# A hand-ordered head for a chunk-selecting attention kernel: first loads as float32 by the SyncE queue, rounding on chip, and zero matmuls on TensorE

## The chip, the cores and the metric

The kernel runs on one core of a Trainium2 chip. A core has five engines with an instruction queue each: TensorE (PE, matmuls; its weight loads are shown as PEld), VectorE (DVE), ScalarE (ACT), GpSimd (POOL) and SyncE (SP). Engines run side by side and wait for one another by semaphores; each engine takes its own instructions in order. DMAs are issued from a queue of POOL or of SP and run on sixteen DMA engines. SBUF is the on-chip memory with 128 partitions, PSUM the memory that matmuls write.

The metric is the time of one execution in microseconds on the device. Before the change the median of three runs is 209.1 us (208.97 to 209.35).

## The reference

Four batches of eight heads, 768 positions, head size 64, all inputs float32. The first half is attention in which each query sees at most six chunks of 32 keys; the second half is a gated MLP over the joined heads.

```python
k_min, k_max = min/max of k over each chunk of 32           # 24 chunks
ub   = sum_d max(q*k_min, q*k_max)                          # upper bound of each query against each chunk
ub   = where(chunk of the query >= chunk, ub, -1e9)
top  = the 6 chunks of largest ub
s    = q @ k.T / 8, kept where the chunk is selected and the key is not later, else -1e9
attn = softmax(s) @ v                                       # per head
x    = heads joined: (4, 768, 512)
h = relu(x @ w_in); u, v = halves of h
v = normalise(v) over its 512 features; v = w_spatial @ v + b_spatial (over positions)
out = (u * v) @ w_out                                       # (4, 768, 512) float32
```

## The kernel before

Two heads make a *pair*; there are 16 pairs, four for each batch. All on-chip operands are float16: the loads of `q`, `k` and `v` go through POOL's DMA queue, which casts from float32 on the way (`load_k`, `load_q`, `load_v`, L318 to L345). A *group* `g` is two pairs that are loaded together; the first group's `k` and `q` are loaded pair by pair (L329, L338), all later ones in one DMA for both pairs (L327, L336).

For each pair the work has these steps, by the names in the code:

- `k_transpose` (L170, six PE transposes, out `kTp`), `k_max` and `k_min` (L178, L182, DVE reductions to 24 chunk bounds), `k_bounds` (L189, two small copies `km<-kmm`), `k_operand` (L194, two copies of the transposed keys into half of `kh`; the other half of `kh` holds a constant pattern, `expand`, that `init_kh` (L150) writes once into each of the eight `kh` tiles).
- `q_transpose` (L205, five PE transposes, out `trm` or `tr`), `q_parts` (L210 and L212 or L214: positive and negative part of q, out `rq`), `bounds` (L219 and L222: `ub`, with the causal mask `later` added by a matmul), `top` (L232: ten MAX8), `select` (L237: writes "not selected" flags into `qs` beside q).
- `a_transpose` and `a_copy` (L251, L257): for each of the two heads, q and flags transposed into the moving operand `a`.
- `scores` (L266, and in batch 0 the diagonal mask `tri` by L269), `e` (L271: exp on ACT), `values` (L289), `normalise` (L296, L297), `x_transpose` (L310, L311). Each pair has two heads of six score tiles: twelve exps, ten of 512 columns and two of 128.

The MLP of a batch runs among the pairs of the next batch (`mlp`, L388 and around).

The order of the work is set by *beats*: `at(beat, step)` puts a step on a list, twelve beats to a pair, and the steps are traced beat by beat. A scheduler then orders each engine's instructions by its own estimates, but inside `tc.manual_schedule` the engines that are named keep the traced order. Before the change this holds for PE alone and for the beats below 6. Beat `B0` (-30) holds the initial work: the first loads, the constants and the whole chain of pair 0 up to its first scores. `p` is pair 0, `n` pair 1. DMAs, POOL's work and everything on DVE and ACT are ordered by the scheduler.

The first work on each queue before the change is, in order: POOL issues two `k` DMAs (pair 0), makes `identity` (L116), issues two `q` DMAs (pair 0), two `k` DMAs (pair 1), makes the masks `later` and `tri` (L140 to L145), and issues the `q` DMAs of pair 1, `v` of group 0, and then `k`, `q`, `v` of group 1. DVE sets zeros (`qs` of all three groups, `km`, `eps_t`, ones in `vt`), then makes `expand` (L132) and `sub_chunk` (L135), and waits for `kTp`. ACT loads its table, writes four of the constant halves of `kh`, works for pair 0, and writes the other four. SP has nothing to do before 60 us.

PSUM: `ml_tile` and `trans_tile` of batch 0 share three buffers of the pool `ps_ml`; `sc` has three buffers of its own.

Of the kernel before, what the change touches and what calls it, by code (L numbers as in the profile page):

```python
# [16 lines left out]
P = 128  # L17
# [31 lines left out]
def kernel(  # L49
# [62 lines left out]
    eps_t = cp.tile([P, 1], F32)  # L112

# [5 lines left out]
    def init_ring(i):  # L119

        nc.vector.memset(qs_ring[i][:, :, :, 0:4:3, :], 0.0)

    def init_small():
        nc.vector.memset(km_ring[0], 0.0)
        nc.vector.memset(km_ring[1], 0.0)
        nc.vector.memset(eps_t, 1e-6)
        for t in v_ring:
            nc.vector.memset(t[:, :, :, D:D + 2], 1.0)

# [8 lines left out]
    def init_masks():  # L138

        nc.gpsimd.memset(later, 0.0)  # L140
# [3 lines left out]
        nc.gpsimd.memset(tri, 0.0)  # L144
# [3 lines left out]
    def init_kh(i):  # L148
        for hi, (d0, d1) in enumerate(HALF):
            nc.scalar.copy(kh_ring[i][hi][d0:d1, :], expand)  # L150
# [6 lines left out]
    class Pair:  # L157
# [27 lines left out]
        def k_bounds(self):  # L185
            for hi, (d0, d1) in enumerate(HALF):
                copy = nc.gpsimd.tensor_copy if 2 <= self.i < 4 else nc.scalar.copy
                s0, s1 = HALF[1 - hi]
                copy(self.km[d0:d1, :, hi], self.kmm[s0:s1])  # L189
# [12 lines left out]
        def q_transpose(self):  # L202
            self.tr = self.trans_tile()
            for t in range(1, NQT):
                nc.tensor.transpose(self.tr[:, t * P:(t + 1) * P], self.qs[:, t, 1:3, :], identity)  # L205

        def q_parts(self, m):
            if m == 0:
                self.rq = sb.tile([P, 2, S], F16, tag="rq", name="rq")
                nc.vector.tensor_scalar(self.rq[:, 0, P:S], in0=self.tr[:, P:S], scalar1=0.0, scalar2=None, op0=Alu.max)  # L210
            elif self.i < 1:
                nc.scalar.activation(self.rq[:, 1, P:S], self.tr[:, P:S], func=Act.Relu, scale=-1.0)  # L212
# [40 lines left out]
        def a_copy(self, hi):  # L253
            if self.i >= 8:
                return
            copy = nc.vector.tensor_copy if self.i < 2 and hi == 0 else nc.scalar.copy
# [60 lines left out]

    def load_k(g, hi, xy=None):  # L318
# [7 lines left out]
        if xy is None:  # L326
            nc.gpsimd.dma_start(out=t[:, :, :, 1 - hi, :].rearrange("p x t d -> p (x t) d"), in_=source(k, b, h, 2))  # L327
        else:
            nc.gpsimd.dma_start(out=t[:, xy, :, 1 - hi, :], in_=source(k, b, h + xy, 1))  # L329

    def load_q(g, hi, xy=None):
# [3 lines left out]
        if xy is None:  # L335
            nc.gpsimd.dma_start(out=t.rearrange("p x t d -> p (x t) d"), in_=source(q, b, h, 2))  # L336
        else:
            nc.gpsimd.dma_start(out=t[:, xy], in_=source(q, b, h + xy, 1))  # L338

    def load_v(g):  # L340
        b, hp = divmod(2 * g, HP)
        t = v_ring[g % 3]
        nc.gpsimd.dma_start(out=t.rearrange("p h t c -> p (h t) c")[:, :, 0:D], in_=source(v, b, 2 * hp, 4))
# [10 lines left out]
    def load_w_in(j):  # L354
        for hi in range(2):
            r = (4 * (j // 2) + j % 2 + 2 * hi) * D
            nc.gpsimd.dma_start(out=w_in_sb[hi * D:(hi + 1) * D, j], in_=moe_w_in[r:r + D, :])
# [96 lines left out]
    at(B0, load_k, 0, 0, 0)  # L454
    at(B0, load_k, 0, 1, 0)
    at(B0, init_identity)
    at(B0, load_q, 0, 0, 0)
    at(B0, load_q, 0, 1, 0)
    at(B0, init_ring, 0)
    at(B0, init_small)  # L460
    at(B0, init_expand)
    at(B0, load_k, 0, 0, 1)
    at(B0, load_k, 0, 1, 1)
    at(B0, init_masks)
    at(B0, load_q, 0, 0, 1)
    at(B0, load_q, 0, 1, 1)
    at(B0, load_v, 0)
    at(B0, init_ring, 1)
    at(B0, init_ring, 2)
    at(B0, init_kh, 0)  # L470
    at(B0, init_kh, 1)
    at(40, load_b)
    for g in range(1, NPAIR // 2):
        t0 = 2 * g * BEATS
        for hi in range(2):
# [3 lines left out]
    for i, p in enumerate(pairs):  # L479
        t0 = i * BEATS  # L480
        for hi in range(2):
            for g in range(len(TILES)):
                at(t0 + 6 * hi + g, p.scores, hi, g)
# [6 lines left out]
    for i, p in enumerate(pairs):  # L490
# [3 lines left out]
        t0 += 4 if i < 4 else 0  # L494
        at(t0 - (22 if i < 4 else 27), p.k_transpose)
# [16 lines left out]
    p, n = pairs[0:2]  # L512
    for beat, *step in (
            (B0 + 1, p.k_transpose), (B0 + 1, p.k_max), (B0 + 1, p.k_min), (B0 + 1, p.k_operand, 0),
            (B0 + 1, p.q_transpose), (B0 + 1, p.q_parts, 0), (B0 + 1, p.k_bounds),
            (B0 + 1, p.q_parts, 1), (B0 + 1, p.k_operand, 1), (B0 + 1, p.bounds), (B0 + 1, p.top, 0),
# [78 lines left out]
```

The softmax here doesn't subtract the row's maximum and nothing guards it: scores larger than these inputs give would overflow.

## Time and profile before

| What | us |
|---|---|
| median of three runs | 209.1 (208.97 to 209.35) |
| the profiled execution, its own time | 208.6 |
| span of that execution, first to last instruction | 206.9 |
| busy in the span: PE / DVE / ACT / POOL | 187.8 / 154.5 / 158.1 / 80.5 |
| first transposes of pair 0 on PE start | 5.75 |
| first exp starts | 15.29 |
| copies of `a` of pair 3 on ACT start (36 exps are done) | 37.91 |
| first MLP activation on ACT starts | 57.10 |

The span is 1.7 us shorter than the execution's time, and the execution is 0.5 us below the median. A busy PE is not a PE at its peak, since matmuls are pipelined and their ends are modelled. In a line of instructions the columns are start, length, engine, line of the code, operation, output and inputs with their shapes, and in brackets the idle time before it with what ended it. In a line of the chain of work that ended last they are start, length, and what it was.

### The profile page before, as it was taken

The page shows a single profiled execution, that of the slowest core. Times are in us where ns is not written, and L with a number is a line of the kernel's source. Part 1 is how long each engine was busy: PE and PEld are TensorE (multiplying, and loading weights), DVE is VectorE, ACT ScalarE, POOL GpSimd, SP SyncE. Part 2 cuts the span into 40 slices and gives each one's busy share as a digit, 9 for nine tenths or more (in the row PEclk, how much of TensorE's full clock was granted, in tenths as well). Part 3 has the DMA queues.
Part 4 walks back from the last instruction along what each step waited for, and adds up shares of the span by engine and source line. Part 5 has one row for each costly group of instructions (what it writes and reads, how often), then busy time and mean ns, then how long its engine had stood idle before and what let it go on. Part 6 is the DMA issues. An engine that isn't in the chain of part 4 may idle for free.

```text
span 206.9 us, 5068 instructions
## 1 busy us (share of the span) xinstructions
PE 187.8 (91%) x1922; PEld 115.1 (56%) x1922; DVE 154.5 (75%) x454; ACT 158.1 (76%) x326; POOL 80.5 (39%) x100
## 2 busy tenths in 40 slices
PE   0368999898899999999999999999999999999992
PEld 0266776775666665656655656565555454444440
DVE  6467979989799989899797999887647456365520
ACT  4797989899998889785989996669999830666042
POOL 7997659596992463236114111111111110000000
PEclk9999999999999999999999999999999999999999
DMA  5999999999999999979998926648782124540356
GB/s 38 92 118 154 140 178 158 173 177 167 177 162 162 97 119 128 135 130 147 149 278 153 180 62 57 127 88 158 181 166 65 38 29 92 187 152 3 72 128 256
DMA packets 114424, 27.27 MB, mean 132 GB/s; under 512 B 109536, under 2 KB 110816, under 8 KB 114400
## 3 DMA queue, kind: packets, MB, share of 16 engines
q0 software_dynamic: 76544, 12.20, 89.8%
q1 hardware_dynamic: 37856, 14.75, 36.4%
q8 instruction: 15, 0.25, 0.5%
q14 instruction: 9, 0.07, 0.1%
HBM read 24.38 MB, written 6.29 MB: 148 GB/s over the span
## 4 chain that ended last, share of the span: by engine, by line
PE 69%; ACT 17%; DVE 8%; issue 2%; DMA 2%; POOL 0%; DVEq 0%; ACTq 0%; POOLq 0%
PE mlp L388 40%; PE sc L266 12%; ACT e L271 10%; PE acc L289 7%; PE kTp L170 2%; ACT a L257 2%; DVE kmm L178 2%; PE ub L222 2%; DMA k<-in_k_dram 2%; PE trm L251 2%; ACT vraw L398 1%; PE tr L205 1%; DVE vn L412 1%; DVE kmm L182 1%; ACT u L420 1%
## 5 line engine op out<-in xcount | busy, mean ns | idle before, releaser
L271 ACT ACTIVATE e<-sc 128x512 f16<-128x512 f32 x192 | 96.9, 553 | 14.8 <-PE sc L266 13.4
L266 PE MATMUL sc<-a,kh 128*128 128x512 f16 (+3 forms) x256 | 65.5, 308 | 2.1 <-ACT e L271 1.5
L388 PE MATMUL mlp<-w_in_sb,xT 128*128 128x512 f16 x192 | 53.0, 379 | 0.1
L278 POOL TENSOR_SCALAR_AFFINE_SELECT e<-e 128x768 f16<-128x768 f16 x24 | 20.9, 869 | 66.3 <-ACT e L271 66.3
L289 PEld LDWEIGHTS <-e 128*128 128x128 f16 x672 | 31.4, 97 | 17.0 <-DVE x L297 3.8
L388 PE MATMUL mlp<-vn,wsT 128*128 128x512 f16 x144 | 37.3, 379 | 0.0
L289 PE MATMUL acc<-vt,e 128*128 128x65 f16 x672 | 35.3, 193 | 0.7 <-DVE x L297 0.4
L266 PEld LDWEIGHTS <-kh 128*128 128x128 f16 x256 | 22.7, 98 | 13.3 <-issue 0.8
L437 ACT COPY o<-mlp 128x512 f32<-128x512 f32 x24 | 14.1, 586 | 19.5 <-PE mlp L388 19.1
L400 DVE BATCH_NORM_STATS2 stats<-vraw 128x6 f32<-128x512 f32 x24 | 16.6, 693 | 12.9 <-ACT vraw L398 12.5
L388 PE MATMUL mlp<-w_out_sb,gT 128*128 128x512 f16 x96 | 25.1, 379 | 0.0
L388 PEld LDWEIGHTS <-xT 128*128 128x128 f16 x192 | 17.2, 97 | 12.6 <-issue 0.4
L427 DVE SCALAR_TENSOR_TENSOR g<-mlp,b_col,u 128x512 f16<-128x512 f32 x24 | 17.9, 748 | 7.3 <-PE mlp L388 6.2
L232 DVE MAX8 max<-ub 128x8 f32<-128x8 f32 (+4 forms) x160 | 15.6, 165 | 5.1 <-PE ub L222 4.9
L388 PEld LDWEIGHTS <-wsT 128*128 128x128 f16 x144 | 12.9, 98 | 10.4
L178 DVE TENSOR_REDUCE kmm<-kTp 128x24 f16<-128x768 f16 x16 | 15.2, 948 | 3.7 <-PE kTp L170 2.7
L297 DVE TENSOR_TENSOR x<-acc,rec 128x384 f16<-128x384 f32 x32 | 17.6, 551 | 0.4
L336 POOL DMA_DIRECT2D qs<-in_q_dram x14 | 14.6, 1049 | 5.9 <-PE sc L266 5.9
L194 DVE COPY kh<-kTp 64x768 f16<-64x768 f16 x30 | 16.5, 549 | 0.5
L398 ACT ACTIVATE vraw<-mlp 128x512 f32<-128x512 f32 x24 | 14.4, 601 | 3.0 <-PE mlp L388 3.0
L420 ACT ACTIVATE u<-mlp 128x512 f16<-128x512 f32 x24 | 14.3, 598 | 1.7 <-PE mlp L388 1.5
L327 POOL DMA_DIRECT2D k<-in_k_dram x14 | 14.4, 1045 | 2.5 <-PE kTp L170 1.8
(67 smaller groups left out, 230.2 us busy)
## 6 DMA issues: line engine op xcount, KB each, us to landing
out_dram<-o SPq DMA_DIRECT2D x24, 256.0 KB, 2.3
vt<-in_v_dram POOLq DMA_DIRECT2D x8, 384.0 KB, 8.8
k<-in_k_dram POOLq DMA_DIRECT2D x14, 192.0 KB, 8.1
qs<-in_q_dram POOLq DMA_DIRECT2D x14, 192.0 KB, 7.5
ws_raw<-in_moe_w_spatial_dram POOLq DMA_DIRECT2D x6, 192.0 KB, 6.9
w_in_sb<-in_moe_w_in_dram POOLq DMA_DIRECT2D x8, 128.0 KB, 6.9
w_out_sb<-in_moe_w_out_dram POOLq DMA_DIRECT2D x4, 128.0 KB, 7.9
k<-in_k_dram POOLq DMA_DIRECT2D x4, 96.0 KB, 3.4
```

The costliest lines, as they stand in the source:

```text
L178: nc.vector.tensor_reduce(self.kmm[:, 0, :], self.kT.rearrange("d (c ch) -> d c ch", ch=CHUNK), axis=AX.X, op=Alu.max)
L194: copy(self.kh[hi][d0:d1], self.kT[d0:d1])
L266: mm(sc[:, col:col + n], lhsT=self.kh[hi][:, t * P:(t + 1) * P], rhs=self.a[:, q0 // P:(q0 + n) // P, hi, :], start=True, stop=not diag)
L271: nc.scalar.activation(out=self.e[hi][:, g * 512:g * 512 + width], in_=sc[:, 0:width], func=Act.Exp, scale=scale)
L278: nc.gpsimd.affine_select(out=blk, in_=blk, compare_op=Alu.is_ge, fill=0.0, base=0, channel_multiplier=-1, pattern=[[0, NQT], [1, P]])
L289: mm(self.av[:, qi, :], lhsT=self.e[hi][:, c:c + P], rhs=self.v[hi][:, t, 0:D + 1], start=first and n == 0, stop=last and n == len(blocks) ...
L297: nc.vector.tensor_tensor(self.x16[:, :, hi, :], in0=self.av[:, :, 0:D], in1=rec.to_broadcast([P, NQT, D]), op=Alu.mult)
L388: mm(st[group][:, 0:cols], lhsT=lhsT, rhs=rhs, start=(j == 0), stop=(j == n - 1))
L398: nc.scalar.activation(st["vraw"][:, ti, :], h, func=Act.Relu)
L400: nc.vector.bn_stats(stats, st["vraw"][:, ti, :])
L420: nc.scalar.activation(st["u"][:, ti, :], h, func=Act.Relu)
L427: nc.vector.scalar_tensor_tensor(g, in0=vs, scalar=b_col[:, ti:ti + 1], in1=st["u"][:, ti, :], op0=Alu.add, op1=Alu.mult)
```

## The change

It changes four things.

1. *First loads.* `k` and `q` of pair 0 are loaded as float32 by SP's queue, one DMA for each head (`load_first`), into two new tiles, and are rounded to float16 on chip: `k` by a DVE copy, `q` by an ACT copy (`round_first`). POOL's queue no longer loads them. The loads of the first three groups and of `w_in` are kept in program order on POOL.
2. *Who does what at the start.* The zeros of `qs` for groups 1 and 2 go from DVE to POOL, the zeros of `later` and `tri` from POOL to DVE. Of the eight constant halves of `kh`, ACT writes three and DVE five, all before the rounding. The negative part of q in pair 0 goes from ACT to DVE. `a_copy` of pair 1, first head, goes from DVE to ACT. `k_bounds` of pairs 2 and 3 goes from POOL to ACT.
3. *Order by hand.* The hand-kept order now covers PE, DVE and ACT, for the beats below 7, and the beats of pairs 0 to 3 are written anew; in pairs 2 and 3 `k_transpose` comes at 18 beats before the pair in place of 22 less 4.
4. *Zeros on PE.* `warm_up(n)` runs n matmuls of zeros, 128x512, into an `ml_tile` that nothing reads: seven before pair 0's `k_transpose`, two after it, two after `q_transpose`, two after pair 1's `k_transpose`.

From pair 4 on every engine has the same instructions in the same order as before, except that POOL no longer copies `km` and its DMA issues stand a few places apart.

```diff
+    zeros = cp.tile([P, 512], F16)
+    k_first = cp.tile([P, 2, NQT, D], F32)
+    q_first = cp.tile([P, 2, NQT, D], F32)
     def init_ring(i):
-        nc.vector.memset(qs_ring[i][:, :, :, 0:4:3, :], 0.0)
+        (nc.vector if i == 0 else nc.gpsimd).memset(qs_ring[i][:, :, :, 0:4:3, :], 0.0)
+    def warm_up(n):
+        out = ml_tile()
+        for _ in range(n):
+            mm(out, lhsT=zeros[:, 0:P], rhs=zeros, start=True, stop=True)
     def init_masks():
-        nc.gpsimd.memset(later, 0.0)
+        nc.vector.memset(later, 0.0)
...
-    def init_kh(i):
-        for hi, (d0, d1) in enumerate(HALF):
-            nc.scalar.copy(kh_ring[i][hi][d0:d1, :], expand)
+    def init_kh(i, hi, engine):
+        d0, d1 = HALF[hi]
+        copy = nc.scalar.copy if engine is nc.scalar else engine.tensor_copy
+        copy(kh_ring[i][hi][d0:d1, :], expand)
...
-                copy = nc.gpsimd.tensor_copy if 2 <= self.i < 4 else nc.scalar.copy
+                copy = nc.gpsimd.tensor_copy if 2 <= self.i < 2 else nc.scalar.copy
...
-            elif self.i < 1:
-                nc.scalar.activation(self.rq[:, 1, P:S], self.tr[:, P:S], func=Act.Relu, scale=-1.0)
...
-            copy = nc.vector.tensor_copy if self.i < 2 and hi == 0 else nc.scalar.copy
+            copy = nc.vector.tensor_copy if self.i < 1 and hi == 0 else nc.scalar.copy
...
+    def load(now, **kw):
+        ins = nc.gpsimd.dma_start(**kw)
+        if now:
+            tc.keep_in_program_order(ins)
...
+    def load_first():
+        for x, t in ((k, k_first), (q, q_first)):
+            for hi in range(2):
+                nc.sync.dma_start(out=t[:, hi if x is q else 1 - hi],
+                                  in_=x[0, pairs[0].heads[hi]].rearrange("(so si) d -> si so d", si=P))
+    def round_first(what):
+        if what == "k":
+            nc.vector.tensor_copy(tiles["k", 0][:, 0], k_first.rearrange("p h t d -> p t h d"))
+        else:
+            nc.scalar.copy(pairs[0].qs[:, :, 1:3, :], q_first.rearrange("p h t d -> p t h d"))
...
+    for beat, *step in (
+        (B0, load_first), (B0, init_identity), (B0, nc.vector.memset, zeros, 0.0), (B0, warm_up, 7),
+        (B0, init_ring, 0), (B0, init_expand), (B0, init_masks),
+        (B0, load_k, 0, 0, 1), (B0, load_k, 0, 1, 1), (B0, load_q, 0, 0, 1), (B0, load_q, 0, 1, 1), (B0, load_v, 0),
+        (B0, init_small),
+        (B0, init_kh, 0, 0, nc.scalar), (B0, init_kh, 0, 1, nc.scalar), (B0, init_kh, 1, 0, nc.scalar),
+        (B0, init_kh, 1, 1, nc.vector), (B0, init_kh, 2, 0, nc.vector), (B0, init_kh, 2, 1, nc.vector),
+        (B0, init_kh, 3, 0, nc.vector), (B0, init_kh, 3, 1, nc.vector),
+        (B0, round_first, "k"), (B0, round_first, "q"),
+        (B0, p.k_transpose), (B0, p.k_max), (B0, p.k_min), (B0, warm_up, 2), (B0, p.q_transpose), (B0, warm_up, 2),
+        (B0, p.q_parts, 0), (B0, p.k_bounds), (B0, p.q_parts, 1), (B0, p.bounds), (B0, p.k_operand, 0),
+        (B0, p.top, 0), (B0, p.top, 1), (B0, p.select), (B0, n.k_transpose), (B0, warm_up, 2), (B0, p.k_operand, 1),
+        (B0, p.a_transpose, 0), (B0, p.a_copy, 0), (B0, p.a_transpose, 1), (B0, n.k_max), (B0, p.scores, 0, 0),
+        (B0, p.a_copy, 1), (B0, n.k_min), (B0, n.q_transpose),
+    ):
+        at(beat, *step)
...
+        if i < 4:
+            for beat, *step in (
+                (18, p.k_transpose), (17, p.k_max), (14, p.k_min), (15, p.q_transpose),
+                (15, p.q_parts, 0), (12, p.q_parts, 1), (12, p.k_bounds), (11, p.bounds),
+                (8, p.k_operand, 0), (9, p.top, 0), (8, p.top, 1), (8, p.select),
+                (7, p.k_operand, 1), (5, p.a_transpose, 0), (5, p.a_copy, 0),
+                (4, p.a_transpose, 1), (4, p.a_copy, 1),
+            ):
+                at(t0 - beat, *step)
+            continue
...
-    with tc.manual_schedule(engines={mybir.EngineType.PE}):
-        for beat in sorted(b for b in beats if b < 6):
+    with tc.manual_schedule(engines={mybir.EngineType.PE,mybir.EngineType.DVE,mybir.EngineType.Activation}):
+        for beat in sorted(b for b in beats if b < 7):
```

On ACT the work between the first exp and the copies of `a` of pair 3 is before the change 36 exps, four small `km` copies and three `a` copies; after it 36 exps, eight `km` copies and five `a` copies (the second head's copy of pair 0 now stands behind the first exp).

## The prediction, written before the result was known

> **What bounds the kernel now.** I read three views. First the busy time of each engine in five stretches, cut where something changes hands (columns: stretch, its length, then busy us and instructions of PE, PEld, DVE, ACT, POOL, then granted clock, DMA share, GB/s):
>
> ```profile
> 0.00:15.29 15.29, 5.26 (x46) 4.13 (x47) 8.86 (x29) 11.15 (x15) 14.10 (x23) 1.00 1.27 81
> 15.29:37.91 22.62, 20.60 (x294) 15.34 (x292) 19.70 (x65) 19.72 (x45) 16.87 (x23) 1.00 2.58 159
> 57.10:160.00 102.90, 102.28 (x1094) 62.82 (x1092) 87.59 (x267) 88.21 (x192) 32.28 (x35) 1.00 1.28 138
> ```
>
> From 57 us PE has work without a gap, and the order there is untouched: whatever the head gains is carried to the end as a shift. Before 15.29 no exp runs, and from there to 37.91 (36 exps done) ACT is busy 19.72 of 22.62 us. So two numbers decide: when the first exp starts, and how long ACT then needs to the copies of `a` of pair 3.
>
> Second, the chain of work that ended last, in its first 16 us:
>
> ```profile
> 1.33 0.45 POOL k L329
> 2.28 3.33 DMA k<-in_k_dram
> 5.75 0.81 PE kTp L170 x6
> 6.58 0.96 DVE kmm L178
> 7.54 0.88 DVE kmm L182
> 8.50 0.79 ACT kh L194
> 9.81 0.71 ACT rq L212
> 10.57 0.56 PE ub L222 x9
> 11.15 0.93 DVE max L232 x10
> 12.56 0.72 PE trm L251 x5
> 13.28 0.64 PE kTp L170 x6
> 13.92 0.64 PE trm L251 x6
> 14.56 0.43 PE sc L266
> ```
>
> The reader sees the load first (until 5.61), then 2.1 us in which ACT copies keys before it makes `rq` (8.42 to 10.57), and at 13.28 PE work of pair 1 among that of pair 0.
>
> Third, the engines' lines in time:
>
> ```profile
> 4.05 0.51 DVE L135 COPY sub_chunk<-identity 128x128 f16<-128x128 f16 x1
> 4.16 3.35 ACT L150 COPY kh<-expand 64x768 f16<-64x768 f16 x4 [2.07 <-DVE expand L132]
> 14.35 0.63 PE L266 MATMUL sc<-a,kh 128*128 128x512 f16 x1
> 18.61 3.21 ACT L271 ACTIVATE e<-sc 128x512 f16<-128x512 f32 x7 [0.77 <-PE sc L266]
> 19.25 0.38 PE L266 MATMUL sc<-a,kh 128*128 128x512 f16 x1
> ```
>
> The same score matmul takes 0.63 us at 14 and 0.38 us at 19, with the granted clock shown as 1.00 throughout: PE is slow until it has been busy for some us, and ACT waits for it.
>
> **The change, step by step.**
>
> *Loads by SP.* Nothing in the trace loads 256-byte rows by SP's queue. SP gets its first instruction like the others near 0.9. It issued two output DMAs in 1.00 us, so I put issues at 0.9, 1.4 (k), 1.9, 2.4 (q). Landing is bounded by SP's own kinds: 2.3 us for an output DMA, 4.7 for the largest transpose. So k is in at 3.7 to 6.1, q at 4.7 to 7.1; I take 4.3 and 5.6, near the 2.5 us of a `gT` transpose with two thirds of the packets. Both are covered, as the next two steps show.
>
> *DVE's queue before the rounding of k.* This replaces the load as the first limit. POOL now first zeros 1536 elements: its two memsets (240 elements 0.357 us, 128 elements 0.263) give 0.84 ns an element, so 1.45 us, from 0.9 to 2.35; `identity` follows (0.32) until 2.7. `expand` on DVE starts at 2.75 (0.41), then `sub_chunk` (0.51) to 3.67, masks and `zeros` by the memset rows (0.10 at 48, 0.70 at 768 words) 0.27 behind it to 3.94, the six small memsets 0.45 (1.77 to 2.22 before) to 4.39. Five constant copies of 64x768: at most 0.83 (ACT's row for the same copy), at least 0.16 (a MAX8 of eight elements); DVE's own row of that size from SBUF, `expand`, is 0.41 and reads repeated elements, so I take 0.3, between it and the floor: 1.5, to 5.9. Rounding 128x768 from float32: 0.75 scaled from `vn` (512 columns, 0.5 apart), 0.5 unscaled; I take 0.65. It ends at R = 6.55 (5.7 to 8.9), against 5.61 for the landed float16 load. k lands before 5.9 in all but the worst case.
>
> *ACT.* Three constant copies (0.84 each) from 3.2 to 5.7, then the rounding of q, 0.8 like its 768-column copies: 6.5, or 7.9 if q is late. PE's `q_transpose` then ends by 8.8 even with two slow zero matmuls of 0.43 ahead of it; it is wanted at R + 2.4 = 8.95. Hidden.
>
> *From R to the first exp.* Transposes 0.49 (a later row) or 0.81 (slow PE); both reductions 1.84; two parts of q on DVE 0.89, with the `km` copies (0.48) beside them and the key copies no longer ahead; `ub` 0.41 or 0.56; max and select 1.35; six transposes 0.5 or 0.85; copy of `a` 0.56; scores with mask to the exp 0.55 or 0.94; seven hand-offs of 0.04. That is 6.9 with a fast PE, 8.1 with a slow one. Pair 1's transposes and two zeros (0.5 + 0.43, slow 0.85 + 0.85) now run while DVE does max and select (1.35): hidden with a fast PE, 0.35 over with a slow one. They wait for pair 1's k, which POOL issues at 4.9 and 5.75 behind 1.45 more memset and two mask selects; with the 3.4 us to landing of such loads it is there at 9.2, wanted at 10.8. The buffer of `a` waits for ACT's two key copies: reductions end 8.95, `km` 0.48, twice 0.79: 11.0, wanted at 11.9. For the zeros: thirteen matmuls, all in waits of PE; I take a third of the slow price, 7.3. First exp: 6.55 + 7.3 = 13.85, 1.4 earlier than 15.29.
>
> *From the first exp to pair 3's copies.* ACT had 19.72 us of work here. Added: four `km` copies (0.24 each, 0.96) from POOL, one `a` copy of pair 1 from DVE and pair 0's own one that moves behind the first exp (0.75 each, 1.5): 22.2. Taken away is waiting: 2.9 us before, of which the profile names 1.2 for transposes of `a` and 1.3 for scores, in part with the slow PE. In the new order the copies stand behind exps whose scores are long done: pair 1's copies follow eight exps, 5 us after the first, its flags are ready at 4.0. I leave 0.4. DVE loses 0.55 and is no limit (19.70 of 22.62 before). POOL no longer blocks its DMA issues behind `km` (2.7 and 1.3 us of waiting): loads come earlier, worth nothing, since nobody waited for them after 8.5. Pair 3's copies: 13.85 + 22.2 + 0.4 = 36.45, against 37.91.
>
> **Sum.** 1.5 us earlier, and from pair 4 on all is shifted: span 206.9 - 1.5 = 205.4, execution 208.6 - 1.5 = 207.1. The median lay 0.5 above that execution: 207.6.
>
> [...] In the row above `sub_chunk`, 128 elements, took 0.51 us while POOL was issuing DMAs, longer than `expand` with 768 elements, and POOL's issue beside `expand` took 1.12 in place of 0.84. [...]
>
> PE's two speeds are in the rows (0.63 and 0.38). [...]
>
> **Rivals.**
>
> *Bigger gain.* Copies at their floor and a fast PE: R = 5.7, first exp 12.6, 0.2 of waiting: 35.0, gain 2.9; the stretch to 57 us has 1.07 us of ACT idle, of which some may go too. 205.4 to 206.6. For it: PE is fed, and no row makes plain copies slow; against it: nothing shows such a copy at 0.16.
>
> *ACT pays it back (slower).* ACT's added 2.5 us are certain, its waits need not vanish: an order by hand cannot adapt, and each `a` copy that waits for PE holds up the exps behind it. If ACT still waits 2.9 us: 13.85 + 22.2 + 2.9 = 38.95, 1.0 later, 210.1. It decides from 1.9 us of waiting on. For it: the three waits of `a` for transposes before; against it: the flags are ready a microsecond ahead.
>
> *DVE's front is late (no change, or slower).* If R is 8.0 or more, because copies cost 0.55 (as from PSUM), POOL's memset holds DVE, or k lands past 7, the first exp is at 15.3 and the end 209.1, and 209.9 at R = 8.8. This is also the case that SP's load does not do its job.
>
> *Loads of group 1.* POOL's issues for it end at 13.85 in place of 15.17, landing up to 7.4 us after issue, near 20.2; PE wants pair 2's q some 6 us after the first exp, 19.9. A stall there costs up to 1.2 us of scores: 208.7.
>
> **How the numbers follow.** Gain of 0.6 to 2.4 us as summed (206.7 to 208.5): 45%. Bigger: 25%. ACT pays back: 12%. Late front: 12%, half of it within the 0.4 us (0.2%) that a measurement can tell from none. Loads: 6%, mostly a small gain. So faster 75%, same 8%, slower 17%. Leaving out the far half of the slow cases and the tip of the big gain, the range is 205.4 to 209.9; it holds cases of both signs, and the likeliest one's own is 206.7 to 208.5.
>
> **What would show it.** First exp on ACT near 13.85; rounding of k ending near 6.55 and starting when DVE is free, not when a DMA lands; constant copies of 0.3 us; score matmuls of 0.38 at the first exp; pair 3's `a` copies near 36.5 with under 1 us of ACT waiting; from there equal distances to the end. Wrong if `k_first` lands past 6, if DVE's copies beside POOL stretch, or if ACT waits on `trm` as before.

## The result, and the profile after

The changed kernel takes 212.16 us (median of four runs, 210.97 to 212.55), the kernel before 209.22 us (four runs, 208.97 to 209.35): a ratio of 1.0132, 95% interval 1.0090 to 1.0175. It is 2.9 us slower. The forecast was 207.6 us, faster; the time lies outside its range of 205.4 to 209.9. The ratios below leave out executions that took over 1.5% longer than the fastest of their kernel; this concerns three of the twelve of g3_head alone, its profiled one among them.

The profiled execution of the changed kernel took 211.94 us, its span is 210.2 us (before: 208.6 and 206.9). First the busy times in stretches cut at the same events as before: first exp, pair 3's copies of `a`, first MLP activation. The columns are stretch, length, busy us and instructions of PE, PEld, DVE, ACT and POOL, granted clock, DMA share, GB/s.

```profile
0.00:14.68 14.68, 9.05 (x59) 4.52 (x60) 11.13 (x36) 6.55 (x9) 13.31 (x19) 0.88 1.18 112
14.68:37.41 22.73, 19.82 (x295) 14.99 (x293) 19.74 (x65) 22.01 (x49) 15.48 (x19) 1.00 2.56 159
59.59:160.00 100.41, 99.02 (x1063) 60.67 (x1062) 85.10 (x260) 84.71 (x183) 30.52 (x32) 1.00 1.32 136
```

The head did gain: first exp 14.68 (15.29 before), pair 3's copies 37.41 (37.91). But the first MLP activation starts at 59.59, not 57.10. Between 37.41 and 59.59, where the prediction had only a shift, a lead of 0.5 us turned into a lag of 2.5; and PE is no longer busy without a gap afterwards (99.02 of 100.41 us).

The chain of work that ended last, of the changed kernel, says through what it went (columns: start, length, what):

```profile
2.54 1.70 DVE expand L141
6.93 0.75 DVE k L362
7.73 0.84 PE kTp L180 x6
...
46.67 0.95 POOL qs L327
47.62 9.41 DMA ws_raw<-in_moe_w_spatial_dram
57.07 0.63 POOL vt L327
57.70 0.82 issue
59.54 0.89 POOL e L286
```

Two things are new. `expand` takes 1.70 us, and from 46.67 to 60.43 the chain runs through POOL's queue: a weight load, then a load that waits for it, then a mask select of `e` (L286) behind both. This is pair 4's second select, at 59.54; its first, at 55.61, is the one that PE is seen to wait for below. POOL's lines in time show the order. Before the change:

```profile
50.84 2.04 POOL L327 DMA_DIRECT2D k<-in_k_dram  x2 [0.67 <-PE sc L266]
52.93 0.86 POOL L278 TENSOR_SCALAR_AFFINE_SELECT e<-e 128x768 f16<-128x768 f16 x1
53.74 1.43 POOL L343 DMA_DIRECT2D vt<-in_v_dram  x1
55.17 0.56 POOL L363 DMA_DIRECT2D w_out_sb<-in_moe_w_out_dram  x1
```

and after it:

```profile
50.91 2.04 POOL L327 DMA_DIRECT2D k<-in_k_dram  x2 [0.66 <-DMA k<-in_k_dram]
52.93 0.57 POOL L389 DMA_DIRECT2D w_out_sb<-in_moe_w_out_dram  x1
54.14 0.55 POOL L389 DMA_DIRECT2D w_out_sb<-in_moe_w_out_dram  x1 [0.64 <-DMA qs<-in_q_dram]
55.07 0.53 POOL L389 DMA_DIRECT2D w_out_sb<-in_moe_w_out_dram  x1 [0.39 <-DMA ws_raw<-in_moe_w_spatial_dram]
55.61 0.88 POOL L286 TENSOR_SCALAR_AFFINE_SELECT e<-e 128x768 f16<-128x768 f16 x1
```

The first mask select of pair 4 (`triangle`, the only compute work of POOL that PE needs in this stretch) starts 2.68 us later, because three more loads of `w_out` stand ahead of it. Two of them wait for older transfers of the same queue to land (0.64 and 0.39 us). PE first uses these weights at 100.6 us. PE and ACT, lines in time, the first one PE's:

```profile
56.54 0.36 PE L297 MATMUL acc<-vt,e 128*128 128x65 f16 x6 [2.69 <-POOL e L286]
57.16 0.60 ACT L279 ACTIVATE e<-sc 128x512 f16<-128x512 f32 x1 [3.30 <-PE sc L274]
```

PE's `values` for the selected `e` waits 2.69 us, and everything behind it on PE's queue waits with it. Among the listed waits of the kernel before, none of PE's is for POOL's `e`. The change text moves none of these instructions: the scheduler, which orders POOL by its own estimates, put the loads there when the work around them changed.

A further 0.7 us went between 90 and 100 us (reductions at 90.48 and 99.77, before at 87.72 and 96.30), at another select of POOL, and some 0.3 us in between.

### The profile page after: what moved, and what is told of

It is laid out like the page before. It is cut to its first block, busy times and chain, and to the rows that moved or that the text cites. A ratio compares the mean times of both kernels' runs of the same rounds, so it can differ in the third digit from the quotient of the medians.

```text
span 210.2 us, 5097 instructions
## 1 busy us (share of the span) xinstructions
PE 191.4 (91%) x1935; PEld 114.9 (55%) x1935; DVE 157.5 (75%) x461; ACT 156.0 (74%) x326; POOL 78.6 (37%) x92
## 4 chain that ended last, share of the span: by engine, by line
PE 58%; ACT 16%; DMA 8%; DVE 7%; POOL 5%; issue 4%; POOLq 0%; ACTq 0%
PE mlp L414 37%; PE sc L274 10%; ACT e L279 9%; PE acc L297 6%; DMA ws_raw<-in_moe_w_spatial_dram 4%; DMA a<-qs 4%; ACT a L265 3%; POOL qs L327 2%; PE kTp L180 1%; DVE vn L438 1%; PE ub L230 1%; ACT vraw L424 1%; PE tr L216 1%; ACT u L446 1%; POOL k L327 1%
## 5 line engine op out<-in xcount | busy, mean ns | idle before, releaser
L286 POOL TENSOR_SCALAR_AFFINE_SELECT e<-e 128x768 f16<-128x768 f16 x24 | 20.8, 868 | 66.4 <-ACT e L279 66.3
L274 PEld LDWEIGHTS <-kh 128*128 128x128 f16 x256 | 22.6, 97 | 13.7 <-DMA a<-qs 0.6
L327 POOL DMA_DIRECT2D qs<-in_q_dram x16 | 16.2, 1023 | 7.5 <-PE sc L274 4.7
L327 POOL DMA_DIRECT2D k<-in_k_dram x16 | 16.3, 1031 | 2.5 <-PE kTp L180 1.8
```

Source lines behind the costliest of these rows:

```text
L274: mm(sc[:, col:col + n], lhsT=self.kh[hi][:, t * P:(t + 1) * P], rhs=self.a[:, q0 // P:(q0 + n) // P, hi, :], start=True, stop=not diag)
L286: nc.gpsimd.affine_select(out=blk, in_=blk, compare_op=Alu.is_ge, fill=0.0, base=0, channel_multiplier=-1, pattern=[[0, NQT], [1, P]])
L327: ins = nc.gpsimd.dma_start(**kw)
```

## The experiments

All are variants of the changed kernel. Unless said otherwise PE, DVE, ACT and SP keep its order to the last instruction. Times are medians; ratios are to the kernel before on the same chip.

### Which GpSimd order, first try: e1_pins

All loads of `w_out`, `w_spatial` and `b` are kept behind the GpSimd instruction traced before them.

```diff
-        nc.gpsimd.dma_start(out=w_out_sb[:, j], in_=...)
+        load(True, out=w_out_sb[:, j], in_=...)      # likewise ws_raw and b_col
```

> The changed kernel with the loads of w_out, w_spatial and b_spatial held in program order on POOL, so that one w_out load instead of four stands ahead of POOL's first mask select of pair 4; PE, DVE and ACT keep the changed kernel's order instruction for instruction. Theory A (the loss is POOL's order: the select waits behind DMA issues that wait for older DMAs, and PE waits for the select): first exp stays at 14.7 and pair 3's copies at 37.4, PE's wait of 2.7 us near 54 falls under 0.6, the time falls by 2.5 to 3 us to about 209.3. Theory B (the shift is lost because the loads themselves land late, or because of the clock of PE): the wait near 54 moves but does not shrink, time stays above 211.3.

Measured: 213.88 us (ratio 1.0238, 1.0206 to 1.0271), slower still. The wait at 57 did go (ACT's `e` at 54.43 after 0.44 us of waiting), but the edit put the sixth load of `w_spatial` behind the selects, issued at 55.00 in place of 47.62, and PE's transposes of these weights have a fixed place in its queue. The waits of PE, e1_pins (engine, line, releaser: us in total, times, longest):

```profile
PE wtr L394 <- DMA ws_raw<-in_moe_w_spatial_dram: 3.8, 1, 3.8
...
PE acc L297 <- POOL e L286: 0.4, 1, 0.4
```

So one wait was exchanged for another of the same kind: the experiment supports the cause and does not give the price. It also shows that this region has little slack in either direction.

### Three heads on that order: e4_both, e3_nozero, e6_pool_load

e4_both also moves GpSimd's second ring memset behind the masks; e3_nozero is e4_both without the 13 zero matmuls; e6_pool_load is e4_both with pair 0's `k` and `q` loaded by GpSimd as float16 again, without the rounding.

```diff
         (B0, init_masks),
+        (B0, init_ring, 2),                          # e4_both: not before the masks
...
-        for _ in range(n):
+        for _ in range(0):                           # e3_nozero
...
-        (B0, load_first),
+        (B0, load_k, 0, 0, 0), (B0, load_k, 0, 1, 0), (B0, load_q, 0, 0, 0), (B0, load_q, 0, 1, 0),   # e6_pool_load
-        (B0, round_first, "k"), (B0, round_first, "q"),
```

> As e1_pins, and POOL's second zeroing of 1536 elements stands behind the two mask selects, all else in the same order. Theory A (expand on DVE is held for the length of POOL's memset): expand takes about 0.5 us instead of 1.70, everything up to the first exp comes 1.1 earlier (13.6), pair 3's copies near 36.4, time 1.0 below e1_pins. Theory B (expand is slow by itself, because it reads one element many times): expand stays at 1.7, no change. Theory C (the head is no longer what sets the end): first exp at 13.6, time as e1_pins.

> As e4_both without any of the thirteen zero matmuls. Theory A (they open PE's clock): score matmuls at the first exp take 0.63 again instead of 0.38, first exp 0.5 to 1.0 later than in e4_both, time 0.5 to 1.2 above it. Theory B (they are worth nothing, since the clock closes again before the transposes): first exp within 0.2, same time. Theory C (they do harm later, as the lower and changing mean clock of the changed kernel suggests): time below e4_both, clock back at 1.00, runs closer together.

> As e4_both, but pair 0's k and q are loaded as float16 by POOL's queue, first of all its work, and nothing is rounded. Theory A (the loads by SP are worth their rounding, since POOL's queue is freed of four issues): pair 1's keys land 3.5 us later, PE's transposes of pair 1 wait for them and hold up pair 0's copies of a; first exp 0.8 to 1.5 later than in e4_both, time 0.5 to 1.5 above. Theory B (the load is hidden behind DVE's constants in both): k is transposed 0.7 earlier because the rounding is gone, first exp up to 0.7 earlier, time the same or less.

Measured: 215.43, 213.89 and 218.49 us (ratios 1.0309, 1.0248, 1.0436), all with the wait of e1_pins for `ws_raw` in them (5.2, 3.8 and 4.0 us). These waits differ by more than the heads do (e3_nozero, whose head is later, ends 1.5 us before e4_both), so that only the heads can be read. In e4_both `expand` is short, as expected, and yet the rounding starts no earlier, because the memset, which now runs at 4.21 to 5.79, falls beside the five copies. DVE's lines in time, e4_both (the third is one of the five copies):

```profile
2.54 0.55 DVE L143 TENSOR_SCALAR expand<-identity 64x768 f16<-64x768 f16 x1 [0.46 <-POOL identity L119]
...
3.74 3.19 DVE L162 COPY kh<-expand 64x768 f16<-64x768 f16 x5
4.48 1.52 DVE L162 COPY kh<-expand 64x768 f16<-64x768 f16 x1
6.96 0.56 DVE L364 CAST k<-k_first 128x768 f16<-128x768 f32 x1
```

3.19 us for five copies, 2.03 in the changed kernel. It is not that each copy is slower: one takes 1.52 us and ends 0.2 us behind the memset, the median of the five is 0.36. The 1.15 us saved on `expand` is paid on that copy, and the first exp stays at 14.66. Without zeros it comes at 15.19, 0.53 later. With GpSimd's loads it comes at 17.57: not because `k` lands late (PE starts its transposes at 5.64), but because `identity` now stands behind four DMA issues, so that `expand` starts at 5.17, takes 1.70 us beside the memset, and the copies end at 10.88. In this order of work the loads on SP's queue are worth 2.9 us of head; no run has GpSimd's loads with `identity` ahead of them.

### The loads put back alone: f1_wout_pinned

Only `w_out` is kept in order, so that one load and not four stands ahead of the select.

```diff
-        nc.gpsimd.dma_start(out=w_out_sb[:, j], in_=moe_w_out[j * P:(j + 1) * P, :])
+        load(True, out=w_out_sb[:, j], in_=moe_w_out[j * P:(j + 1) * P, :])
```

> The changed kernel with one thing put back: GpSimd issues one load of w_out, not four, ahead of its first mask select of pair 4 (each later one is pinned behind the GpSimd instruction traced before it); the loads of w_spatial stand where the changed kernel has them, and TensorE, VectorE, ScalarE and SyncE have the changed kernel's order to the last instruction. Theory A (the loss is the select that stands behind DMA issues waiting for older transfers, on the one queue of GpSimd): the head is as in the changed kernel (first exp 14.7, pair 3's a copies 37.4); the wait of ScalarE at 57 (3.3 us) and of TensorE for the selected e (2.7 us) fall to what the kernel before has (below 0.5), the first vraw comes at 56.6 to 57.2, not 59.6, no wait for ws_raw appears, and the time is 212.2 - 2.7 = 209.5, within 208.6 to 210.0. Theory B (the changed head disturbs the clock or the loads of the whole run, and the wait at 56 is only where the slack shows): the wait goes but the time stays at 211 to 212, with a granted clock still at 0.98 to 0.99.

Measured: 208.83 us (208.39 to 209.24, ten runs); ratio 0.9989, 0.9978 to 1.0001. Against the changed kernel's 1.0132 that is 1.4%, or 3.0 us, for the place of the `w_out` loads (GpSimd's other issues moved by a few places with them). GpSimd's lines in time, f1_wout_pinned:

```profile
50.64 0.57 POOL L327 DMA_DIRECT2D w_out_sb<-in_moe_w_out_dram  x1
51.20 0.90 POOL L286 TENSOR_SCALAR_AFFINE_SELECT e<-e 128x768 f16<-128x768 f16 x1
```

The select is 4.4 us earlier than in the changed kernel, the 2.69 us of PE are gone, ACT's `e` follows at 54.19 (0.44 of waiting), the first vraw at 56.63. The head is the changed kernel's (first exp 14.59, pair 3's copies 37.32), and the recorded clock (0.989) is as low as in the changed kernel (0.988): theory A holds, theory B falls. But 0.6 us of lead at pair 3 should then give 208.4, and the span is 206.9 us, exactly that of the kernel before.

### What holds VectorE at the start: f2_ring_after_v and f4_copies_later

f2_ring_after_v moves the second ring memset farther back, behind the first load of `v`; f4_copies_later also moves the five copies behind the rounding. In both, as in g3_head and g4_copies_act further on, the loads of `w_spatial` are kept behind that of `b`.

```diff
         (B0, load_v, 0),
+        (B0, init_ring, 2),
...
-        (B0, init_kh, 1, 1, nc.vector), ... (B0, init_kh, 3, 1, nc.vector),     # f4: five steps moved
         (B0, round_first, "k"),
         (B0, round_first, "q"),
+        (B0, init_kh, 1, 1, nc.vector), (B0, init_kh, 2, 0, nc.vector),         # f4: others later
```

> f1_wout_pinned with GpSimd's second ring memset (1.4 us) moved from ahead of the masks to behind the first load of v; the loads of w_spatial are kept behind the load of b, so that they do not drift into the gap. TensorE, VectorE and ScalarE keep their order. Theory (a VectorE operation of SBUF to SBUF in its fast form and a GpSimd operation hold each other up): expand falls from 1.70 to about 0.5 us, and this time the five copies stay at 0.40 each, since the memset no longer runs beside them (with the memset right behind the masks they took 0.64 each, and nothing was won): the rounding of k starts at 5.8 to 6.0 instead of 6.93 and the first exp comes at 13.4 to 13.8 instead of 14.7. If the gain is kept through pair 3, the time is 1.0 below f1_wout_pinned; if ScalarE's stretch or the load of pair 1 takes it back, pair 3's a copies stay at 37.4 and the time is that of f1_wout_pinned. Rival (expand is slow for its operands, the identity fresh from GpSimd, or for its place): expand stays at 1.7 and nothing moves.

> f2_ring_after_v with VectorE's five kh copies moved out of the way of the rounding of k: two behind it, one behind q's second part, one behind the selection, one between pair 1's maxima and minima, all where VectorE idled (0.92, 0.64 and 0.55 us) in the traces so far. The rounding of k then starts when k has landed (4.3 to 4.9) or VectorE is through its small memsets (3.8), whichever is later: ready at about 5.5, 0.9 before f2_ring_after_v. If k's landing set the head, the first exp comes at 12.6 to 13.0; q, landed at 6.3 and rounded by 7.1, does not hold it, because TensorE takes q after k's reductions. If q or the moved copies hold it, 13.3 or more. The time falls by 0.8 against f2_ring_after_v if the gain is kept to pair 3's a copies, and is the same if not.

Measured: 208.65 us (0.9987, 0.9976 to 0.9998) and 208.46 us (0.9982, 0.9959 to 1.0006); first exps 14.77 and 14.71. Neither differs from f1_wout_pinned, and both first exps are later than the theories had them: each time one VectorE instruction is stretched. DVE's lines, f2_ring_after_v:

```profile
3.73 2.02 DVE L162 COPY kh<-expand 64x768 f16<-64x768 f16 x5
5.79 1.84 DVE L367 CAST k<-k_first 128x768 f16<-128x768 f32 x1
```

and f4_copies_later (the third line is the first of the two copies):

```profile
5.04 0.56 DVE L367 CAST k<-k_first 128x768 f16<-128x768 f32 x1 [1.32 <-DMA k_first<-in_k_dram]
5.63 2.56 DVE L162 COPY kh<-expand 64x768 f16<-64x768 f16 x2
5.63 2.19 DVE L162 COPY kh<-expand 64x768 f16<-64x768 f16 x1
```

The copies of f2_ring_after_v are back at 0.40 on average, as expected, but now the rounding takes 1.84 us in place of 0.56, or, if that is done by 5.60, the first copy behind it takes 2.19 in place of 0.35. No memset runs there. What does run on GpSimd is the issue of the loads of pair 1's `q` (6.16 to 8.04 in f2_ring_after_v, 6.00 to 7.65 in f4_copies_later). That this issue is what holds VectorE is not shown, and two rows speak against it. In the changed kernel the same issue begins 0.37 us after the rounding, just as in f2_ring_after_v, and the rounding takes 0.74 us, there and in f1_wout_pinned. DVE's line and GpSimd's, the changed kernel:

```profile
6.93 0.74 DVE L362 CAST k<-k_first 128x768 f16<-128x768 f32 x1
7.30 1.65 POOL L327 DMA_DIRECT2D qs<-in_q_dram  x2
```

And in f4_copies_later two further copies beside issues of `k` and of `v` (at 10.74 and 14.80) take 0.35 each, though copies of g3_head beside later issues take 0.52 to 1.00. So for the memsets the theory holds as far as `expand` and the copies go (0.55 and, on average, 0.40 us without one beside them; 1.70 in the changed kernel and 0.64 in e4_both with one); whether the form of the VectorE operation matters is not shown, and what stretched the rounding and the copy here is open.

### Are the zeros worth anything: f3_nozero

```diff
-        (B0, warm_up, 7),
...
-        (B0, warm_up, 2),                            # three times; on f1_wout_pinned
```

> f1_wout_pinned without the 13 matmuls on zeros; all other orders stay. If the zeros are worth what the clock of the head shows, the first exp comes 0.3 to 0.8 later than in f1_wout_pinned, pair 3's a copies as much later, and the time is 0.3 to 0.8 longer. If ScalarE's stretch or another wait hides it, the first exp moves and pair 3's a copies do not. If the zeros only delay (they stand in TensorE's queue ahead of transposes that are ready), the first exp comes earlier without them.

Measured: 208.51 us (0.9987, 0.9977 to 0.9997), no later than with zeros, where 0.3 to 0.8 us were expected. But the first exp is 0.75 later (15.34) and pair 3's copies 1.16 later (38.48). The lag of 1.16 us, kept up to 86 us, is 0.50 at the reductions near 96 us (96.99 against 96.49) and 0.24 at the last output copy (203.57 against 203.33). Together with the lead that f1_wout_pinned lost, this pointed at one place. GpSimd's lines in time, f1_wout_pinned, then PE's behind them, then GpSimd's loads in f3_nozero:

```profile
92.30 2.06 POOL L327 DMA_DIRECT2D qs<-in_q_dram  x2 [4.58 <-PE sc L274]
94.35 0.88 POOL L286 TENSOR_SCALAR_AFFINE_SELECT e<-e 128x768 f16<-128x768 f16 x1
```

```profile
95.29 0.36 PE L297 MATMUL acc<-vt,e 128*128 128x65 f16 x6 [0.48 <-POOL e L286]
```

```profile
91.94 2.06 POOL L327 DMA_DIRECT2D qs<-in_q_dram  x2 [3.07 <-PE sc L274]
```

Pair 8's select stands behind two loads of `q`, which wait until 92.30. The releaser named is a PE matmul, but in f3_nozero, where PE runs 1.15 us later, these loads come at 91.94, earlier. Another wait fits: SP's transposing DMAs read `qs`, the tile that the load overwrites. The last of these was issued at 86.44 in f1_wout_pinned and 87.59 in f3_nozero and took 5.2 and 3.7 us to land by the DMA view, so at 91.64 and 91.29, and in both the loads come 0.65 us after that. So at this place the time is set by a DMA and not by the head. Why it landed later in one than in the other is open, and so is where the last 0.26 us of the lag went.

### The second select freed: g1_qs_after_select and g2_nozero_qs

The two loads of `q` (of group 7, used some 30 us later) are queued behind pair 8's second select, and the load of `v` of group 6 is held behind its first, where f1_wout_pinned had it too. g2_nozero_qs is the same without the zeros.

```diff
+    def behind_select(now, hi):
+        return tc.issue_after(selects[8, hi]) if now else nullcontext()
...
+            with behind_select(g == 7, 1):
+                load(g < 3, out=t.rearrange("p x t d -> p (x t) d"), in_=source(q, b, h, 2))
...
+        with behind_select(g == 6, 0):
+            load(g < 3, out=t.rearrange("p h t c -> p (h t) c")[:, :, 0:D], in_=source(v, b, 2 * hp, 4))
```

> f1_wout_pinned with one move on GpSimd: the two loads of q of group 7 are queued behind pair 8's second mask select, not ahead of its first (q of group 7 is first used some 30 us later). In f1_wout_pinned these two loads stood at 92.30 to 94.36, waiting until then for SyncE's transposing DMA of an earlier pair, and the select behind them came at 94.35, so that TensorE idled 0.48 us at 95.29. Theory (the head start of 0.6 us at pair 3's a copies is lost at this second place on the same queue): the select comes at 92.5 to 93.3, the wait at 95 goes, and the time is 0.4 to 0.6 below f1_wout_pinned: 208.2 to 208.4, ratio to the kernel before 0.996 to 0.997. Rival (the transposing DMAs or the ends of the run set the time by then): the wait goes, the next one opens elsewhere, and the time stays within 0.2 of f1_wout_pinned.

> g1_qs_after_select without the 13 matmuls on zeros. Without them f3_nozero was 1.16 us later than f1_wout_pinned from pair 3's a copies to 86 us, and not later at the end, because the select of pair 8 came earlier there. If the head is carried to the end once that select no longer stands behind q's loads, this run ends 0.8 to 1.2 us after g1_qs_after_select (209.1 to 209.5). If something else resynchronises the run (a DMA of SyncE, the last stage), both end within 0.3 us of each other.

Measured: g1_qs_after_select 208.06 us (0.9978, 0.9959 to 0.9998), g2_nozero_qs 208.85 us (1.0021, 1.0001 to 1.0041). GpSimd's lines, g1_qs_after_select:

```profile
91.60 0.86 POOL L288 TENSOR_SCALAR_AFFINE_SELECT e<-e 128x768 f16<-128x768 f16 x1 [3.79 <-ACT e L281]
92.42 1.45 POOL L333 DMA_DIRECT2D vt<-in_v_dram  x1
96.26 0.85 POOL L288 TENSOR_SCALAR_AFFINE_SELECT e<-e 128x768 f16<-128x768 f16 x1 [2.40 <-ACT e L281]
97.08 2.04 POOL L333 DMA_DIRECT2D qs<-in_q_dram  x2
```

The select now waits only for its exp; no wait of PE for GpSimd is listed any more, and PE is busy 20.00 of 20 us from 80 to 100. Pair 3's copies are at 37.41, 0.50 ahead of the kernel before, and the median is 0.59 below it: the lead arrives. That the wait is gone and the lead kept is what the trace shows, with the last output copy at 202.53 against 203.05 before. The times alone do not: the interval of the ratio overlaps that of f1_wout_pinned, and the ratios differ by only 0.2 us, where 0.4 to 0.6 were forecast and the rival had 0.2 at most. And the zeros, which moved pair 3's copies by 0.67 us here (38.08 without), now move the time by 0.79, close to the 0.8 to 1.2 expected. In these runs the rule "what the head gains is carried to the end" holds where both selects are free, and not in f1_wout_pinned and f3_nozero, where the second is not.

### Using the head: g3_head and g4_copies_act

Both start from g1_qs_after_select with the second ring memset behind the first load of `v`. g3_head moves all five VectorE copies to later places on VectorE. g4_copies_act leaves three of them ahead of the rounding, while `k` is on its way, and gives two to ScalarE, where it idled.

```diff
         (B0, init_kh, 1, 1, nc.vector), (B0, init_kh, 2, 0, nc.vector), (B0, init_kh, 2, 1, nc.vector),
-        (B0, init_kh, 3, 0, nc.vector), (B0, init_kh, 3, 1, nc.vector),
         (B0, round_first, "k"), (B0, round_first, "q"),
+        (B0, init_kh, 3, 0, nc.scalar),
...
         (B0, p.k_operand, 1),
+        (B0, init_kh, 3, 1, nc.scalar),
```

> g1_qs_after_select with the head relieved: GpSimd's second ring memset behind the first load of v, and all five VectorE kh copies moved behind q's second part (one behind it, one behind the selection, one between pair 1's maxima and minima, two behind the minima), so that none of them runs beside GpSimd's issues of pair 1's loads, where one copy took 2.19 us in f4_copies_later. The rounding of k runs at 5.0 to 5.6, the reductions of pair 0 start at 6.4 to 6.6 (8.35 in f1_wout_pinned), the first exp comes at 12.7 to 13.3 if nothing else holds it (14.59 there); if q's rounding (7.1) or the clock holds it, 13.6 to 14.2. If the head is carried to the end, the time is as much lower than g1_qs_after_select: 206.6 to 207.4; if it is not, within 0.3 of it.

> g1_qs_after_select with the head relieved in another way than g3_head: GpSimd's second ring memset behind the first load of v, and two of VectorE's five kh copies on ScalarE, where it idled (one behind the rounding of q, one behind pair 0's operand copies); the other three stay on VectorE ahead of the rounding of k, in the time in which k is still on its way. VectorE, busy without a gap from 8.6 to 21 us in g1_qs_after_select, so gets no work back later, as it did in g3_head. Theory (VectorE's chain from k's landing through pair 1 sets the head, and the head is carried to the end): the rounding of k runs at 5.0 to 5.8, the reductions start at 6.5 (8.60), the first exp comes at 12.7 to 13.2 (14.68), pair 3's a copies at 35.6 to 36.4 (37.41), and the time is 1.0 to 1.8 below g1_qs_after_select. Rivals: VectorE's rounding of k is held beside GpSimd's issues of q's loads, as in f2_ring_after_v (it ends at 7.6, and nothing is won); or the granted clock falls to 0.5 in a stretch of the head, as in g3_head and f4_copies_later, and gives back 0.5 to 1.5 us (208.0 to 209.0).

Measured: g3_head 210.02 us (all twelve runs, 208.12 to 211.99; ratio 1.0043, 1.0014 to 1.0072), slower than either outcome expected for it; g4_copies_act 206.98 us (0.9929, 0.9902 to 0.9955), faster than both kernels. The profiled execution of g3_head is its slowest, so that its lines show where it waits and not what this costs on average. In it the first exp is early (13.87), but VectorE is the limit behind it. Its lines, g3_head, with PE's wait for the last of them:

```profile
9.18 1.69 DVE L162 COPY kh<-expand 64x768 f16<-64x768 f16 x1
...
15.69 1.53 DVE L162 COPY kh<-expand 64x768 f16<-64x768 f16 x2
17.25 0.49 DVE L224 TENSOR_SCALAR rq<-trm 128x640 f16<-128x640 f16 x1
17.80 0.22 PE L234 MATMUL ub<-km,rq 128*128 128x48 f16 x1 [3.05 <-DVE rq L224]
```

The first copy met the memset (9.23 to 10.65 on GpSimd) and took 1.69; the last two delayed pair 1's parts of `q`, PE waited 3.0 us for them, and pair 3's copies came at 39.75. In g4_copies_act no copy of VectorE is held. Its lines, with ScalarE's below:

```profile
2.54 0.55 DVE L143 TENSOR_SCALAR expand<-identity 64x768 f16<-64x768 f16 x1 [0.46 <-POOL identity L119]
...
3.74 1.09 DVE L162 COPY kh<-expand 64x768 f16<-64x768 f16 x3
5.05 0.56 DVE L374 CAST k<-k_first 128x768 f16<-128x768 f32 x1 [0.22 <-DMA k_first<-in_k_dram]
6.22 0.96 DVE L192 TENSOR_REDUCE kmm<-kTp 128x24 f16<-128x768 f16 x1 [0.60 <-PE kTp L184]
```

```profile
7.13 0.83 ACT L162 COPY kh<-expand 64x768 f16<-64x768 f16 x1
...
10.20 0.83 ACT L162 COPY kh<-expand 64x768 f16<-64x768 f16 x1
12.61 0.60 ACT L283 ACTIVATE e<-sc 128x512 f16<-128x512 f32 x1 [1.58 <-PE sc L281]
```

The rounding waits for `k` and for nothing else, the first exp is at 12.61, pair 3's copies at 35.43, 2.0 ahead of g1_qs_after_select, and the profiled execution ends 1.7 us before that kernel's (206.18 to 207.84). The twelve runs lie in two groups of six, 205.99 to 206.50 and 207.47 to 208.49 us (the kernel before: 208.28 to 209.26), and the profiled one is of the lower group. So the lead of 2.0 us is carried nearly whole in that execution, while the ratios put g4_copies_act 1.0 us below g1_qs_after_select, the lower end of what was expected. What divides the groups is open.

## Why the prediction was wrong

**The step that failed** is the first sentence of the sum: "1.5 us earlier, and from pair 4 on all is shifted", with its companion in ACT's step, "loads come earlier, worth nothing, since nobody waited for them after 8.5". It looked for who waits for a load and not for who stands behind its issue. GpSimd's queue holds the loads and the mask selects, the selects feed PE, and the scheduler, not the kernel, orders that queue. "The order there is untouched" was read off PE, DVE and ACT; GpSimd's differed by a few places, and those places cost 3.0 us (f1_wout_pinned) and the lead of 0.5 to 0.6 us itself (f1_wout_pinned against g1_qs_after_select). None of the rivals had this mechanism; the 17% for slower were given to others.

**Loads by SP.** Right within its bounds. In the changed kernel the DMA view has the issues at 0.8 and 1.3 (`k`), 1.9 and 2.5 (`q`), and landings 2.8 to 3.2 and 3.6 us later: at most 4.5 and 6.1, where 4.3 and 5.6 were taken. Where something waits for them, `k` is in at 5.04 to 5.25 and `q` at 6.2 to 6.6. Hidden in the changed kernel, as said.

**DVE's queue before the rounding.** The mechanism was right (this queue, and not the load, is the limit), its size wrong: R = 7.67, not 6.55. `expand` 1.70 for 0.41 (+1.29), five copies 2.03 for 1.5 (+0.53), rounding 0.74 for 0.65 (+0.09); the start (-0.21) and the small work between (-0.59) were shorter. The 0.41 was the row of the kernel before, where GpSimd issued DMAs beside `expand` and no memset ran there; the row that spoke against it (`sub_chunk`, 0.51) stands beside the same issues and shows no memset either. In the runs `expand` is 0.55 when no memset of GpSimd runs beside it and 1.70 when one does, and then it ends 0.41 us after that memset (2.45 to 3.83 in the changed kernel, 5.03 to 6.46 in e6_pool_load), as if it began only there. A copy is 0.35 (the median of the five in the changed kernel) or, beside a memset, 1.52 (e4_both) and 1.69 (g3_head). The R of 8.0 from which the rival of a late front was reckoned is shown by no run: with the memset beside `expand` it was 7.67 (changed kernel). Whether VectorE was held by GpSimd's DMA issues in f2_ring_after_v and f4_copies_later is not shown. With the memset and two copies out of its way (g4_copies_act) VectorE ends the rounding at 5.61 and the first exp comes at 12.61: the head of the rival of a bigger gain, reached with copies of 0.35 and not of 0.16.

**From R to the first exp.** 7.0 us against 7.3: right. A third of the slow price was taken for PE's clock, and so it was in the profiled execution: in the changed kernel pair 0's transposes take 0.82 (slow), pair 1's 0.49 (fast) at 11.50, and the scores 0.38. The place where PE becomes fast is not fixed by the order of the work: with that same order of PE's work the two are 0.59 and 0.51 in f1_wout_pinned and 0.82 and 0.81 in f2_ring_after_v; the first exps (14.59 and 14.77) differ little. Without zeros PE is still slow at 15.64 (0.63 for the same matmul), and the first exp is 0.67 later (g2_nozero_qs). What the first seven zeros do is not settled: the first transposes behind them take 0.82 after 3.41 us of idle PE in the changed kernel and 0.59 after 3.23 in f1_wout_pinned, 0.51 after 1.17 in g4_copies_act and 0.82 after 1.16 in f4_copies_later. With all thirteen zeros PE is fast by 11.5 in the changed kernel, though in f4_copies_later its first scores are slow again (0.59 at 13.98). No run has only some of them, so which of them matter is not shown.

**From the first exp to pair 3's copies.** 22.73 us against 22.6: right, with 0.72 us of ACT idle. ACT did not pay the head back.

So the head's own forecast, 36.45, missed by 0.96: 1.11 from R, -0.28 from R to the first exp, 0.13 behind it. With both selects free the rule of the shift then gives 208.65 - 0.50 = 208.15 us, and g1_qs_after_select measured 208.06.

## What to carry to other kernels

Before "the rest is only shifted" is written down, go through every queue that a scheduler orders, those that only issue DMAs included, and ask which compute instruction on it feeds the bottleneck and what may land ahead of it; here loads of `w_out` that nobody needed for 45 us still cost their issue (0.53 to 0.57 us each), and two of them a wait for an older transfer (0.64 and 0.39), to the select behind them. Where a head is to be shortened, first make sure that the lead arrives: one select here cost 3.0 us, and a second swallowed a lead of 0.6 us and over half of a lag of 1.2. And work moved on an engine that is busy without a gap was moved into somebody's way (g3_head, where PE waited 3.05 us for it); on an engine that idled, two copies of 0.83 us cost nothing that the trace shows (g4_copies_act).

## What was not expected of the hardware

Where `expand` or a copy ran beside a GpSimd memset, one VectorE instruction took 1.15 to 1.35 us longer: `expand` 1.70 (changed kernel) for 0.55 (e4_both, with no memset beside it), one copy 1.52 for 0.35 (e4_both, where the other four take 0.35 to 0.56), one copy 1.69 (g3_head). Not every instruction did: beside the memset at 9.43 to 10.83 in f2_ring_after_v a reduction took 0.95 and the two parts of `q` 0.48 each, as in the changed kernel without one. A stretch of the same kind, 1.84 for 0.56 on the rounding (f2_ring_after_v) and 2.19 for 0.35 on a copy (f4_copies_later), came without a memset. GpSimd was issuing DMAs then; but beside other such issues VectorE lost between nothing and 0.65 us, so that the cause is open.

A granted clock of 1.00 in the records did not show that PE was fast in the head. In the changed kernel the record is 0.50 from 8 to 10 us and in g1_qs_after_select 1.00, with the same order of work there and the same slow durations (six transposes 0.82 at 7.7, two zeros 1.06 at 8.35, five transposes 0.74 at 9.20) and the first exp at 14.68 in both. In these runs the durations of equal matmuls (0.63 or 0.38 us for one score tile) tell the speed.
